# A new written order for a one-core transformer block: loads of x and Wk first, turns of Wq later, five reciprocals on ScalarE

## The chip, the core and the metric

The kernel runs on one core of a Trainium2 chip. A core has five engines that each work through their own list of instructions and meet only at semaphores: TensorE (PE in the profile; its weight loads are PEld), VectorE (DVE), ScalarE (ACT), GpSimd (POOL) and SyncE (SP), which here issues most of the DMAs. An engine's DMA issues are marked with a q (SPq, ACTq). SBUF is the on-chip memory, PSUM the eight banks into which TensorE writes. The metric is the time of one execution in microseconds (us).

## The reference

One block of a transformer over 2048 tokens of width 640. The first half is linear attention with a feature map, the second a gated MLP; both have a layer norm ahead and a residual behind.

```python
x = A_x
h = x + _A_ref(_layernorm(x), A_wqkv, A_w_phi, A_wo)
h2 = h + _B_ref(_layernorm(h), B_w_gate, B_w_up, B_w_down)

# _A_ref, 32 heads of width 20
pq = einsum("bhsd,hdf->bhsf", q, w_phi);  pk = einsum("bhsd,hdf->bhsf", k, w_phi)
phi_q = concat([softmax(pq), softmax(-pq)]);  phi_k = concat([softmax(pk), softmax(-pk)])
kv = einsum("bhsf,bhsd->bhfd", phi_k, v);  z = einsum("bhsf->bhf", phi_k)
o = einsum("bhqf,bhfd->bhqd", phi_q, kv) / (einsum("bhqf,bhf->bhq", phi_q, z)[..., None] + 1e-6)
return o.transpose(0, 2, 1, 3).reshape(B, S, D) @ wo

# _B_ref, F = 1536
return ((x @ w_gate) * (x @ w_up)) @ w_down
```

## The kernel before

The tokens are 16 tiles of 128. Every operation has a name, a letter or two and the tile's number, and the text uses these names:

- Loads: x0, x1, x3 (one tile each), x4, x6 and so on (two tiles); wk0 to wk4, wv0 to wv4 (rows of Wk and Wv, 160 KB each), w5 (the feature matrix w_phi, in 40-byte rows), wo0 and wo2 (Wo), wg and wu (rows of the MLP's gate and up weights, 384 KB each), wd0 to wd3 (quarters of the down weights, 480 KB each). All at line 282.
- Turns, which are DMAs that transpose: wqt0 to wqt4 turn Wq out of DRAM (line 306), xt turns a normalized tile of x (465), qT the features of Q (569), oT an attention output (606), hT a normalized tile of h (640). A turn's target has the layout that TensorE needs; what waits for it is the matmul that reads it. Only SP issues turns.
- The start: WT0 to WT4 turn the rows of Wk on TensorE (386, with copies WTe at 248), xt0 and xt1 turn the first two tiles of x there (456, copies xte). Ph0 to Ph2 on POOL spread w_phi to a block form Phi (374). F1_0 to F1_4 fold Phi into Wk on TensorE (405; copies Fe1 at 248), F0_0 to F0_4 do the same for Wq, once the five turns of Wq have landed. A fold of Wk needs its row's turn and all of Phi; a fold of Wq needs all five turns.
- The first half: K, V and Q are the projections (476; of tiles 0 and 1 in five parts, one for each row of the weight, as K1_0), with exponentials Kx (488) and Qx (545, 547), sums Ks (492) and Qs (550), Ln and Exp for the softmax on ACT (495, 497, 553, 560) and products Kn (512) and Qn (564) on POOL. KV is the sum over tokens (520). After the last KV, N multiplies the turned Q features with it (582); then dd (596) makes the denominator, rd (599) its reciprocal, o (602) divides, oT turns, and O multiplies with Wo (612). h (618) adds the residual, hc (626 or 627) centres it, hT turns it.
- The second half: tokens in five blocks of 256, 512, 512, 512 and 256 columns. U{block}_{tile of F}_{gate or up} are the matmuls (655), g (660) copies the gate, u (663) multiplies, D (674) is the down matmul, y (686) adds the residual, w (688) stores. L1n (437) and L2v (633) are small steps of the two layer norms.

What sets the order is a list written out by hand, or rather by a search: `PLAN` gives each operation a number on the scale of us, optionally another engine, and the PSUM banks or buffer slots that it takes. Each engine runs its operations in the order of these numbers, and waits on semaphores for what an operation reads and for the last users of the slot that it takes. A number is an order, not a time: nothing in the kernel reads a clock.

```python
k, a, o.slots = PLAN.get(name, (key, 0, ()))
...
for o in sorted(G.ops, key=lambda o: (o.key, o.i)):
    order[o.eng].append(o)
```

Two PSUM banks hold a projection, an N or an O. A matmul group that takes banks waits until the engine that reads them for the group before is done: exponentials for K and Q, o for N, h for O.

Of the kernel before, what the change touches and what calls it, by code (L numbers as in the profile page):

```python
# [54 lines left out]
WTe1:6.125:1 L1s3:6.193 xt0:6.33::0 wqt0:6.41 WT2:6.609::2 ekz:6.705 L1e1:6.71 xte0:6.808 xn1:6.98::1 WT3:7.046::3 F1_1:7.325::4 WTe2:7.391 L1a3:7.51 WTe3:7.619
WT0:7.646::6 wv0:7.72:1 L1l3:7.976 WT4:8.096::7 WTe0:8.123:1 wv1:8.2 L1e3:8.303 F1_2:8.375::0 Fe1_1:8.396 WTe4:8.573:1 L1n3:8.582 wv2:8.68:1 F1_0:8.694::2
Fe1_2:8.981 xt1:9.013::6 wv4:9.16:1 Fe1_0:9.211:1 F1_3:9.292::4 xn3:9.721::2 xte1:9.795 F1_4:9.863::0 K0_0:10.182::2 L1s5:10.251 xt3:10.359 Fe1_3:10.379
K0_1:10.453 K1_0:10.724::6 Fe1_4:10.963:1 K1_1:10.995 L1s4:11.038 K1_2:11.266 K0_2:11.537 x2:11.547:1 x10:11.669 K0_3:11.808 L1a5:11.825 L1a4:11.948 L1s7:12.057
# [4 lines left out]
L1e6:19.159 Kx3_0:19.252::2 L1s11:19.392 L1n6:19.439 rqz:19.663 V5:19.67::0 Kn0:19.7 Kx3_1:19.836 wqt4:20.023 L1a11:20.302 xn6:20.411::2 Kx5_0:20.42::3
L1s8:20.941 Kx5_1:21.004 V4:21.026::2 xt6:21.333 Kr1:21.588 L1s10:21.728 Ke1:21.879 Sz:22.013 Ve5:22.025::3 L1n7:22.192 K2:22.382::6 Kn1:22.416 L1a10:22.638
x14:22.643 xn7:22.747::0 L1l10:22.871 Ve4:23.053::4 L1a8:23.277 xt7:23.385 L1a9:23.386 Ks3:23.495::2 F0_0:23.738::4 Kx2_0:23.938::4 F0_4:24.057::0 V2:24.376::2
Kx2_1:24.522 x12:24.695 L1e10:25.106 wd0:25.175 Fe0_0:25.199 Ks2:25.258::3 V6:25.732::6 L1l8:25.783 L1e8:26.109 Ve2:26.202::5 L1n9:26.389 L1n8:26.613
L1n11:26.651:1 Kr2:26.786 L1s15:26.826 mk0:26.837 mk1:27.001 Ke2:27.077 K4:27.088::4 Fe0_4:27.223 mk2:27.346 Ve6:27.613:1:6 Kn2:27.616 xn8:27.807:1:1
xn9:28.344::3 KV0:28.444::2,3 Kr3:28.622 F0_2:28.777::0 xn11:28.874::2 Kx4_0:28.975::0 xt9:28.982 KV1:29.096 Ks5:29.404::0 K7:29.429::6 Kx4_1:29.559
L1n10:29.929 Ke3:30.143 Fe0_2:30.289 xt8:30.292 Kn3:30.477 KV2:30.785 Ks4:30.797::1 Kr5:30.916 Kx7_0:31.062::1 F0_3:31.118::4 V7:31.437::0 wu1:31.602
Kx7_1:31.646 wg0:32.082 L1s12:32.19 Kr4:32.309 wu0:32.562 Ke4:32.6 Fe0_3:32.746 K6:32.793::6 Kn4:32.934 xt11:33.042 L1a12:33.1 Ks7:33.209::3 Ve7:33.33::7  # L70
# [4 lines left out]
KV5:41.933 K11:42.266::0 Qx0_1:42.328 Qr1:42.938::0 L1e12:43.084 Ke9:43.177 L1n12:43.322:1 Kr8:43.323 L1n13:43.364 Qx5_0:43.469::2 Qb1:43.588 xn12:43.606::3
Q3:43.622::4 L1n14:43.787 Kn9:44.011 Qx5_1:44.079 L1n15:44.136:1 xn15:44.42::1 Kx11_0:44.689::3 Qs0:44.95 KV6:44.989 xt15:45.058 Kx11_1:45.273 Q9:45.322::6
Ke8:45.857 Qe1:46.003 Qx3_0:46.122::3 Qn1:46.324 wg2:46.368 Ks11:46.385::2 KV7:46.689 Qx3_1:46.732 wo0:46.848 K10:47.022::0 Qx9_0:47.342::4 Kn8:47.589
xn13:47.778::2 Qx9_1:47.952 Qs5:48.308 V8:48.378::4 xt13:48.416 Kr11:48.562 Qr0:48.708::1 Kx10_0:48.854::4 Ke11:49.438 Kx10_1:49.584 wg3:49.726 K15:49.734::6
# [8 lines left out]
Kn14:69.394 qT2:69.464::5 KV11:69.761 Qx10_0:69.959::2 V15:70.094::0 Qx10_1:70.569 wd1:70.954 Qs10:71.364 KV12:71.45 Ve15:71.65::6 Qb4:71.707 KV13:71.783
KV14:72.116 Qe4:72.234 Qr13:72.353::3 KV15:72.449 Qn4:72.541 Q6:72.782::6 KVe1:72.98 KVe0:73.23 Qb13:73.806 N0:74.149::4 Qx6_0:74.347::4 N2:74.482::0
qT4:74.673::1 dd0:74.68::0 Q7:74.815::2 rd0:74.895 Qx6_1:74.957 dd2:75.185::1 o0:75.309::0 rd2:76.064 oT0:76.177::0 N1:76.182::6 Qx7_0:76.38::3 o2:76.478::1
Q11:76.515::4 Qr10:76.99::0 Qe13:77.136 dd1:77.233::0 Qx7_1:77.255 Qn13:77.443 rd1:77.448 oT2:77.487::1 o1:77.862::2 Q8:77.882::0 Qx11_0:78.08::5 Qs7:78.617  # L90
Qx11_1:78.69 Qb10:78.708 oT1:78.797::2 N3:79.249::2 Qx8_0:79.494::0 N9:79.582::6 O0:79.915::4 Qe10:80.104 qT13:80.107::5 dd9:80.113::0 Qx8_1:80.223 rd9:80.328
dd3:80.618::1 rd3:80.833 Qr7:80.833::1 o9:81.123::0 Qb7:81.177 O2:81.273::0 Qe7:81.452 Qn7:81.759 o3:81.878::1 oT9:81.991::3 N5:82.631::6 h2:82.83 Q14:82.964::2
qT7:83.301::0 h0:83.65 L2q2:83.775 O1:84.331::0 Qs6:84.47 hc0:84.615::1 oT3:84.791::0 Qx14_0:85.333::1 O9:85.689::4 dd5:85.905::0 Qx14_1:85.943 h1:86.011
hT0:86.101 Qr6:86.553::2 rd5:86.831 Qb6:86.897 Q12:87.047::2 Qe6:87.172 h9:87.246 hc1:87.291::2 Qn6:87.479 o5:88.066::2 hT1:88.147 N4:88.414::0 Qx12_0:88.612::3
# [821 lines left out]
```

## Time and profile before

| | us |
|---|---|
| median of 3 runs | 273.67 (273.38 to 274.04) |
| the profiled execution | 272.24 |
| span of its trace | 270.5 |
| TensorE busy | 264.9 |
| DVE busy | 161.3 |
| ACT busy | 123.8 |
| POOL busy | 71.1 |
| granted TensorE clock | 1.00 |

The span runs from the first to the last instruction in the trace, and times within a trace count from its start. In a timeline a row is start, length, engine, line, operation, target from sources, shape and count; rows of one kind are merged, and a bracket tells for how long the engine was idle before and what ended that. Matmuls overlap, so their lengths add up to more than the time they take, and the distance of two starts is the better measure. In the chain of work that ended last a row is start, length and what the time went to; a DMA's row there runs from its issue to its landing. In rows of DMA issues the last two numbers are the size and the median time from issue to landing. In rows by windows the columns are the window, its length, busy time of PE, PEld, DVE, ACT and POOL with the count of instructions, the granted clock, the DMA engines' share and GB/s. In rows by groups they are the count, then busy us and mean ns of one, then idle time before.

### The profile page before, as it was taken

What the parts mean: (1) busy time and instruction counts of PE and PEld (TensorE: products, weight loads), DVE (VectorE), ACT (ScalarE), POOL (GpSimd) and SP (SyncE); (2) the same over time, 40 slices, a digit from 0 to 9 for tenths busy, and PEclk for the clock granted to TensorE, in tenths of its full rate; (3) what the DMA queues carried; (4) which work ended last, traced back from release to release, by engine and by line L of the source; (5) the groups of instructions that cost most, each with busy time, mean ns of one, the idle gap of its engine ahead of it and who ended that gap; (6) DMA issues with size and microseconds to landing.
All of it is one profiled execution on the core that took longest, in us unless ns stands there. A gap on an engine that the chain in (4) does not pass through costs nothing.

```text
span 270.5 us, 5202 instructions
## 1 busy us (share of the span) xinstructions
PE 264.9 (98%) x2105; PEld 177.9 (66%) x2105; DVE 161.3 (60%) x299; ACT 123.8 (46%) x307; POOL 71.1 (26%) x87
## 2 busy tenths in 40 slices
PE   7899999999999999999999999999999999999996
PEld 4677777777777788567456577766445467544775
DVE  4998999997789799786653434321324322333424
ACT  3799989988766564417406512440120400032000
POOL 4217889999832422330001000000000000000000
PEclk9999999999999999999999999999999999999999
DMA  6998791999979989586253205001300000200003
GB/s 169 326 200 156 178 231 54 172 263 263 199 172 156 137 163 183 104 139 118 52 121 68 55 0 76 23 4 48 73 0 15 0 0 27 73 1 0 27 0 109
DMA packets 67944, 28.09 MB, mean 104 GB/s; under 512 B 59088, under 2 KB 66640, under 8 KB 67920
## 3 DMA queue, kind: packets, MB, share of 16 engines
q1 hardware_dynamic: 66544, 26.12, 47.0%
q10 hardware_dynamic: 1376, 1.64, 2.0%
q8 instruction: 16, 0.26, 0.4%
q14 instruction: 8, 0.07, 0.1%
HBM read 11.00 MB, written 2.62 MB: 50 GB/s over the span
## 4 chain that ended last, share of the span: by engine, by line
PE 94%; DMA 2%; SPq 1%; ACT 1%; issue 0%; DVE 0%; DVEq 0%
PE ps L655 38%; PE ps L476 24%; PE ps L674 19%; PE ps L612 8%; PE ps L520 2%; PE ps L582 2%; DMA ev<-in_A_wqkv_dram 2%; PE ps L405 1%; DMA xnT<-xn 1%; PE ps L386 1%; SPq L306 0%; ACT ph L545 0%; SPq L282 0%; DVE Wp L686 0%; PE ps L456 0%
## 5 line engine op out<-in xcount | busy, mean ns | idle before, releaser
L655 PE MATMUL ps<-xnT,Wgu 128*128 128x512 bf16 (+1 forms) x600 | 108.1, 336 | 0.4 <-DMA xnT<-xn 0.4
L655 PEld LDWEIGHTS ps<-xnT,Wgu 128*128 128x128 bf16 x600 | 58.0, 98 | 43.8 <-issue 0.6
L660 ACT ACTIVATE gt<-ps 128x512 bf16<-128x512 f32 (+1 forms) x60 | 29.4, 509 | 103.1 <-PE ps L655 81.9
L476 PE MATMUL ps<-Wp,xnT 128*128 128x320 bf16 (+1 forms) x480 | 68.4, 299 | 0.0
L663 DVE TENSOR_TENSOR ev<-ps,gt 128x512 bf16<-128x512 f32 (+1 forms) x60 | 33.6, 578 | 55.3 <-PE ps L655 37.0
L476 PEld LDWEIGHTS ps<-Wp,xnT 128*128 128x128 bf16 x480 | 45.7, 97 | 17.3
L674 PE MATMUL ps<-Wd,ev 128*128 128x320 bf16 (+2 forms) x396 | 53.7, 295 | 0.0
L674 PEld LDWEIGHTS ps<-Wd,ev 128*128 128x128 bf16 x396 | 38.2, 98 | 15.0 <-DVE ev L663 0.2
L512 POOL TENSOR_TENSOR ek<-ek,SR 128x1280 bf16<-128x1280 bf16 x16 | 37.6, 2356 | 1.3 <-ACT SR L497 1.1
L686 DVE SCALAR_TENSOR_TENSOR Wp<-ps,rs,x_all 128x640 bf16<-128x640 f32 (+3 forms) x18 | 14.5, 808 | 30.3 <-PE ps L674 29.9
L550 DVE TENSOR_REDUCE S<-ph 128x66 f32<-128x1320 bf16 x16 | 24.2, 1520 | 2.4 <-ACT ph L547 2.3
L492 DVE TENSOR_REDUCE SR<-ek 128x64 f32<-128x1280 bf16 x16 | 23.4, 1467 | 1.0 <-ACT ek L488 0.9
L612 PE MATMUL ps<-Wo,Wp 128*128 128x320 bf16 x160 | 23.9, 299 | 0.0
L545 ACT ACTIVATE ph<-ps 128x600 bf16<-128x600 f32 x32 | 21.3, 689 | 5.3 <-PE ps L476 4.3
L564 POOL TENSOR_TENSOR ph<-ph,RQ 128x660 bf16<-128x660 bf16 x16 | 20.8, 1305 | 9.4 <-ACT RQ L560 9.4
L488 ACT ACTIVATE ek<-ps 128x640 bf16<-128x640 f32 x32 | 21.3, 717 | 0.8 <-PE ps L476 0.7
L612 PEld LDWEIGHTS ps<-Wo,Wp 128*128 128x128 bf16 x160 | 15.4, 98 | 6.7 <-issue 0.3
L618 DVE SCALAR_TENSOR_TENSOR x_all<-ps,x_all 128x640 bf16<-128x640 f32 x16 | 13.1, 822 | 7.5 <-PE ps L612 7.4
L629 ACT ACTIVATE ek<-x_all,mv 128x640 bf16<-128x640 bf16 x16 | 13.1, 820 | 3.5 <-DVE x_all L618 3.5
L602 DVE TENSOR_TENSOR o<-ps,sm 128x660 bf16<-128x660 f32 x16 | 13.3, 838 | 0.4
L248 ACT ACTIVATE ev<-ps 128x640 bf16<-128x640 f32 x13 | 9.2, 713 | 1.5 <-PE ps L476 1.4
L557 POOL TENSOR_TENSOR RQ<-RQ 128x32 f32<-128x32 f32 x14 | 3.3, 239 | 24.5 <-ACT RQ L553 24.4
(66 smaller groups left out, 164.0 us busy)
## 6 DMA issues: line engine op xcount, KB each, us to landing
out_dram<-Wp SPq DMA_DIRECT2D x15, 160.0 KB, 1.8
x_all<-in_A_x_dram SPq DMA_DIRECT2D x6, 320.0 KB, 4.5
...
Wp<-in_A_wqkv_dram SPq DMA_DIRECT2D x5, 160.0 KB, 4.1
ev<-in_A_wqkv_dram SPq DMA_DIRECT2D x4, 160.0 KB, 4.0
x_all<-in_A_x_dram ACTq DMA_DIRECT2D x3, 160.0 KB, 3.4
```

Of the source, the lines that this page charges most:

```text
L476: ins = e.matmul(pb(b, hb)[:, 0:n1 - n0], lhsT=T["xnT"][:, NC - 1 - c, P * t:P * (t + 1)], rhs=T["Wp"][:, POS[kind], c, n0:n1], start=(c = ...
L488: G.op("act", "%sx%d_%d" % (nm, t, s), lambda e, s=s, b=b, ek=ek: e.activation(out=T["ek"][:, ek.slots[0], 0:2 * D].rearrange("p (b h s f) ...
L492: G.op("dve", "%ss%d" % (nm, t), lambda e, ek=ek, sr=sr: e.tensor_reduce(out=T["SR"][:, sr.slots[0], 0, :], in_=T["ek"][:, ek.slots[0], 0: ...
L512: G.op("pool", "Kn%d" % t, lambda e, eng, ek=ek, sr=sr: e.tensor_tensor(out=T["ek"][:, ek.slots[0], 0:2 * D].rearrange("p (h f) -> p h f", ...
L545: e.activation(out=v[:, 0:10].rearrange("p (b g) j f -> p b g j f", b=2), in_=pp(b, 0, 300).rearrange("p b (g j f) -> p b g j f", j=3, f=D ...
L550: G.op("dve", "Qs%d" % t, lambda e, t=t, ph=ph: e.tensor_reduce(out=T["S"][:, t, 0:66].rearrange("p (g k) -> p g k", k=6), in_=pv(ph).rear ...
L564: return e.tensor_tensor(out=v, in0=v, in1=T["RQ"][:, rq.slots[0], 1, 0:33].rearrange("p (g j) -> p g j", j=3).unsqueeze(3).to_broadcast([ ...
L612: ins = e.matmul(pb(b, hb)[:, 0:320], lhsT=T["oT"][:, oT.slots[0], c, :], rhs=T["Wo"][:, c, 320 * hb:320 * (hb + 1)], start=(c == 0), stop ...
L655: ins = e.matmul(pb(b)[:, 0:n], lhsT=T["Wgu"][:, gu, c, P * ft:P * (ft + 1)], rhs=T["xnT"][:, NC - 1 - c, o0:o0 + n], start=(c == 0), stop ...
L660: G.op("act", "g%d_%d" % (bi, ft), lambda e, pg=pg, gt=gt, n=n: e.activation(out=T["gt"][:, gt.slots[0], 0:n], in_=pb(pg)[:, 0:n], func=AF ...
L663: o_ = G.op("dve", "u%d_%d" % (bi, ft), lambda e, pu=pu, gt=gt, hh=hh, ft=ft, n=n: e.tensor_tensor(out=T["hh"][:, hh.slots[0], ft, 0:n], i ...
L674: ins = e.matmul(pb(b, hb)[:, 0:w], lhsT=T["hh"][:, hh.slots[0], ft, P * tt:P * (tt + 1)], rhs=T["Wd"][:, ft, c0 + w * hb:c0 + w * (hb + 1 ...
```

## The change

The whole list `PLAN` is replaced, so that nearly every engine has another order; the matmuls, their shapes and their number stay. What the text speaks of:

- SP's first issues were wqt2, w5, x3, wk2, wk3, wk0, wk4, wv3, x4, x6, wqt0, wv0, wv1, wv2, wv4, xt3; they are x3, wk0, x1, wk1, w5, wk3, wk4, wk2, wv2, x4, wv0, x2, wv1, x6, x10, wv3, xt3, wv4, wqt2, wqt0. ACT issued x0, x1, wk1 and later x2, wo2 and wd2; it issues x0 and later wd0. The turns of Wq were at 0.8, 6.4, 12.6, 17.3 and 20.0 on the list's scale; they are at 10.3, 11.6, 16.8, 19.4 and 20.7.
- TensorE had WT1, xt0, WT2, WT3, F1_1, WT0, WT4, F1_2, F1_0, xt1, F1_3, F1_4, K0_0. It has WT0, WT1, WT3, xt0, WT2, WT4, F1_1, xt1, F1_0, F1_2, F1_4, F1_3, K1_0. The five copies Fe1 were four on ACT and one on DVE and are all on ACT; xte0 and xte1 go from ACT to DVE.
- On POOL an L1n stands between Ph0 and Ph1; several memsets go from the start to after 15.
- Wd's loads were at 25, 71, 97 and 133 and are at 32 (wd3), 58 (wd0, on ACT), 59 (wd2) and 71. xt8 stands right behind wo0 and wd3.
- Where the first half ends, TensorE had N0, N2, Q7, N1, Q11, Q8, N3, N9, O0, O2; it has N0, N2, Q7, N9, N1, Q11, N3, Q8, O0, Q14, O2. SP had hT2, qT14, oT10, hT4, hT5 ahead of block 1's first U; it has hT2, hT5, qT14, hT4, oT10.
- The reciprocal of the denominator goes from DVE to ACT for tiles 2, 5, 6, 14 and 15, as Ln and Exp of minus that. The 33rd column of the result, which is padding, is set to zero once by POOL.

```diff
+RACT = (2, 5, 6, 14, 15)
...
-gl0:0.78 wqt2:0.78 x0:0.78:1 va1:0.846 zero:0.91 warm0:1.127 x1:1.26:1 warm1:1.345 warm2:1.564 eps:1.676 id0:1.706 wk1:1.74:1 warm3:1.782 id1:1.944 warm4:2.001
-w5:2.09:1 gla:2.188 warm5:2.219 phz:2.398 warm6:2.437 x3:2.57:1 warm7:2.656 warm8:2.874::0 wk2:3.05:1 warm9:3.093 glb:3.115 warm10:3.311 warm11:3.529 wk3:3.53
...
+x3:0.78:1
...
+wk0:1.26:1
...
+w5:2.7:1
...
+F1_1:8.754::6
...
+wqt2:10.25
...
+wd3:32.33
...
+xt8:32.81
...
+hT5:99.514
...
+    init["sm"] = [G.op("pool", "smz", lambda e: e.memset(T["sm"][:, :, 1, H:H + 1], 0.0), 0.1, LP, [], [], -60.2)]
...
-        G.op("dve", "rd%d" % t, lambda e, sm=sm: e.reciprocal(out=T["sm"][:, sm.slots[0], 1, 0:33], in_=T["sm"][:, sm.slots[0], 0, 0:33]),
-             0.30, LD, [sm], [sm], kk)
+        if t in RACT:
+            G.op("act", "rl%d" % t, lambda e, sm=sm: e.activation(
+                out=T["sm"][:, sm.slots[0], 0, 0:H], in_=T["sm"][:, sm.slots[0], 0, 0:H], func=AF.Ln), 0.24, LA, [sm], [sm], kk)
+            G.op("act", "rd%d" % t, lambda e, sm=sm: e.activation(
+                out=T["sm"][:, sm.slots[0], 1, 0:H], in_=T["sm"][:, sm.slots[0], 0, 0:H], func=AF.Exp, scale=-1.0), 0.21, LA,
+                [sm], [sm], kk)
+        else:
+            G.op("dve", "rd%d" % t, lambda e, sm=sm: e.reciprocal(
+                out=T["sm"][:, sm.slots[0], 1, 0:33], in_=T["sm"][:, sm.slots[0], 0, 0:33]), 0.30, LD, [sm], [sm], kk)
```

More of the change, by code (lines that the diff above doesn't have):

```diff
@@ L55 @@
[L55 to L58, printed above, removed]
@@ L63 @@
[L63 to L66, printed above, removed]
@@ L67 @@
[L67 to L70, printed above, removed]
@@ L75 @@
[L75 to L78, printed above, removed]
@@ L87 @@
[L87 to L94, printed above, removed]
@@ new lines @@
+warm0:1.127
+warm1:1.345
+warm2:1.564
+warm3:1.782
+warm4:2.001
+warm5:2.219
+warm6:2.437
+warm7:2.656
+id0:0.78
+id1:1.018
+warm8:2.874::0
+warm9:3.093
+x3:0.78:1
+L1s3:3.725
+x0:0.78:1
+L1s0:4.512
+warm10:3.311
+warm11:3.529
+L1a3:5.299
+warm12:3.748
+warm13:3.966
+warm14:4.185
+warm15:4.403
+wk0:1.26:1
+WT0:4.846::1
+warm16:5.404
+warm17:5.622
+warm18:5.82
+gl0:1.262
+x1:1.74
+wk1:2.22
+WT1:6.096::2
+w5:2.7:1
+L1a0:5.422
+WTe0:5.602
+eps:1.329
+gla:1.425
+glb:1.728
+L1l0:6.187
+L1s1:5.531
+L1l3:6.369
@@ new lines @@
+L1a1:6.441
+ekz:1.938
+Ph0:6.225
+warm19:6.375
+warm20:6.484
+warm21:6.593
+L1e0:6.551
+xn0:6.789::0
+L1e3:6.695
+L1n3:6.975
+xn3:7.319::1
+WTe1:6.788:1
+L1l1:7.373
+L1e1:7.699
+xn1:7.937::2
+wk3:3.18
+WT3:7.146::0
+wk4:3.66:1
+xt0:7.456::3
+Ph1:7.199
+wk2:4.14:1
+WT2:8.196::4
+xte0:8.467:1
+WTe3:7.792:1
+WT4:8.475::5
+WTe2:8.673
+Ph2:7.591
+F1_1:8.754::6
+Fe1_1:9.271
+WTe4:8.952:1
+xt1:9.073::1
+xte1:9.55:1
+wv2:4.62:1
+x4:5.1
+L1s5:9.959
+F1_0:9.352::2
+F1_2:9.671::4
+Fe1_0:9.869:1
+Fe1_2:10.453:1
@@ new lines @@
+F1_4:10.032::6
+wv0:5.58:1
+F1_3:10.351::0
+Fe1_3:11.037
+L1s4:10.745
+Fe1_4:11.621:1
+L1a5:11.533
+L1a4:11.655
+K1_0:10.67::2
+K1_1:10.941
+K0_0:11.214::4
+x2:6.06
+L1s2:11.764
+wv1:6.54
+x6:7.02
+L1l4:12.205
+x10:7.5
+K0_1:11.485
+K0_2:11.756
+L1e4:12.531
+L1n5:12.769:1
+xn5:13.053::3
+K1_2:12.027
+K1_3:12.298
+wv3:7.98
+K1_4:12.569
+Kx1_0:13.039::0
+Kx1_1:13.623
+L1n4:12.811
+xn4:13.583::0
+xt3:8.46
+wv4:9.77:1
+L1a2:14.113
+L1l2:14.346
+L1e2:14.672
+L1n2:14.952
+wqt2:10.25
+K0_3:12.84
+K0_4:13.111
@@ new lines @@
+L1s6:14.222
+Ks1:15.009::0
+V1_0:13.382::0
+Kx0_0:14.765::1
+Kx0_1:15.349
+xn2:15.933:1:2
+wqt0:11.56
+va1:15.176
+xt5:13.691
+L1a6:16.402
+V0_0:13.653::6
+L1s7:16.511
+L1a7:17.421
+V0_1:13.924
+V0_2:14.195
+V1_1:14.466
+V1_2:14.737
+mk0:16.006
+mk1:16.17
+mk2:16.515
+L1s11:17.53
+K3:15.008::2
+Kx3_0:16.748::2
+Kx3_1:17.332
+V1_3:16.364
+phz:16.785
+xt4:15.001
+V1_4:16.635
+x8:16.311
+L1s10:18.317
+L1l6:17.916
+L1e6:18.242
+L1n6:18.522
+xn6:19.104::1
+wqt3:16.791
+V0_3:16.906
+V0_4:17.177
+L1a10:19.634
@@ new lines @@
+L1n7:18.746
+Kr1:18.335
+Ke1:18.626
+L1a11:19.743
+Kn1:18.97
+xt2:18.101
+Ks3:19.852::1
+V3:17.448::4
+Ve3:19.004::0
+L1l10:19.976
+L1e10:20.302
+Ve0:20.395::1
+L1n11:21.245:1
+L1n10:21.283
+wqt4:19.411
+Ve1:20.979::2
+K5:18.804::2
+Kx5_0:21.563::3
+Kx5_1:22.147
+V5:20.16::4
+wqt1:20.721
+xt6:22.031
+V4:21.516::6
+Ks0:21.42::2
+xn7:22.813::3
+xt7:23.451
+Ve4:23.072::3
+Kr0:23.656
+Ke0:23.947
+x12:24.761
+Ve5:24.093::4
+Kn0:24.281
+K2:22.872::0
+Kx2_0:24.677::4
+Kx2_1:25.261
+V2:24.228::2
+F0_4:25.584::6
@@ new lines @@
+Fe0_4:26.101
+Ve2:26.685::5
+F0_0:25.903::4
+V6:26.222::0
+xn11:23.343::0
+KV0:27.578::6,7
+L1s8:23.873
+wu0:25.241
+L1s9:24.66
+L1a9:25.57
+x14:25.721
+L1a8:25.679
+xn10:27.269:1:2
+L1l8:28.084
+Kr3:28.266
+Ks2:25.997::3
+Kr2:28.412
+Ke2:28.703
+L1e8:28.849
+L1n8:29.129
+xt10:28.222
+Ve6:27.778:1:6
+K4:27.911::2
+Fe0_0:28.942
+Kx4_0:29.526::1
+Kx4_1:30.11
+KV1:29.267
+L1n9:29.353
+Ks5:28.509::0
+xn9:29.902::1
+Sz:29.577
+xt9:30.54
+F0_2:29.6::0
+Fe0_2:30.694
+Ke3:31.278
+xn8:30.432::3
+K7:29.919::4
@@ new lines @@
+Kx7_0:31.475::0
+L1s13:30.962
+Kr5:32.059
+Kx7_1:32.205
+rqz:29.756
+wo0:31.85
+V7:31.275::2
+Ks4:31.749::2
+Ve7:32.831::7
+Ke5:33.415
+Kn2:29.793
+KV2:32.631
+F0_3:32.964::0
+L1s12:33.142
+Kr4:33.561
+Ke4:33.852
+Kn3:32.106
+Fe0_3:33.998
+K6:33.283::4
+Kx6_0:34.839::4
+Kx6_1:35.423
+F0_1:34.639::2
+wd3:32.33
+Fe0_1:36.007
+L1s15:33.929
+Ks7:34.716::3
+Kr7:36.591
+Ke7:36.882
+KV3:34.958
+Ks6:36.159::1
+K9:35.291::0
+L1a15:37.552
+Kx9_0:37.028::2
+Kx9_1:37.612
+Q1_0:36.647::4
+Q1_1:36.919
+Q1_2:37.191
@@ new lines @@
+Qx2_0:54.834::5
+Qx2_1:55.444
+Qs9:54.605
+qT5:54.824::1
+K13:54.636::4
+Kx13_0:56.192::1
+Kx13_1:56.776
+xt14:56.314
+Kr15:57.36
+Ke15:57.651
+Qs2:56.239
+Qr2:57.797::0
+Qb2:58.099:1
+Qn3:58.332
+KV9:55.992
+Kn15:59.597
+Qr9:57.943::1
+V10:56.325::0
+qT0:57.624::2
+wd0:58.089:1
+V11:57.681::2
+Ve10:58.569::5
+Ks13:59.599::0
+Ve11:59.237::0
+wd2:59.114
+K12:59.037::4
+Kx12_0:60.593::2
+Kx12_1:61.177
+KV10:60.393
+KV11:60.726
+Kr13:61.761
+Ke13:62.052
+Q4:61.059::0
+Qx4_0:62.624::0
+Qx4_1:63.234
@@ new lines @@
+KV13:72.273
+qT9:66.034::4
+Qs4:70.159
+Qr4:71.712::2
+Qs13:71.594
+Qb4:72.182
+Ve15:72.14::7
+KV14:72.606
+wg1:67.524
+KV15:72.939
+KVe0:73.47
+KVe1:74.059
+Qe4:72.724
+Qn4:73.031
+qT2:69.939::5
+Q6:73.272::4
+Qx6_0:74.837::3
+N0:74.639::2
+dd0:75.17::0
+Qx6_1:75.447
+rd0:75.385
+N2:74.972::0
+dd2:75.675::1
+Q7:75.305::6
+N9:76.672::4
+wd1:71.429
+o0:75.799::0
+qT4:75.163::2
+rl2:76.057
+rd2:76.367
+o2:76.672::1
+N1:77.005::2
+dd9:77.427::0
+dd1:77.536::2
+rd1:77.751
+oT0:76.667::0
+o1:78.165::2
@@ new lines @@
+Qr13:76.527::3
+Qb13:76.871
+Qe13:77.146
+Qn13:77.453
+Q11:77.569::0
+oT2:77.977::1
+N3:79.062::2
+Qx7_0:77.265::4
+Qx7_1:77.875
+Qx11_0:79.134::5
+qT13:79.287::5
+rd9:78.92
+Qx11_1:79.744
+Qs7:79.21
+Qr7:80.763::1
+oT1:80.777::2
+Qr10:80.909::0
+o9:80.793::0
+oT9:82.087::3
+Qb7:81.107
+Qs6:81.548
+Qe7:81.382
+Qn7:81.689
+Q8:79.395::6
+Qx8_0:81.501::0
+Qx8_1:82.111
+Qr6:83.101::2
+Qb6:83.445
+Qe6:83.72
+qT7:83.397::4
+O0:80.799::0
+dd3:82.983::0
+rd3:83.198
+o3:83.612::1
+Q14:82.157::4
+oT3:84.887::0
@@ new lines @@
+Qx15_1:98.049
+hT2:97.819
+Qs15:98.844
+u0_1:100.278
+u0_2:100.609
+hc5:98.659::1
+hT5:99.514
+U0_4_0:98.504::0
+L2v1:97.626
+g0_4:100.73::3
+qT14:100.825::1
+N10:99.05::4
+O4:99.383::2
+h4:100.941
+hc4:101.885:1:2
+U0_3_0:100.742::7
+g0_3:101.486::1
+hT4:102.459
+L2r1:102.338
+dd10:102.407::2
+U0_3_1:101.287::6
+U0_4_1:101.834::1
+u0_3:102.513
+u0_4:102.844
+rd10:103.175
+o10:103.59::2
+oT10:104.457::0
+Qr15:101.76::1
+Qb15:102.103
+U0_5_0:102.379::0
+Qe15:102.379
+Qn15:102.686
+qT15:105.767::2
@@ L143 @@
+w15_2:267.08
+smz:29.758
 """.split():
```

686 lines of the change are left out of this document (620 added, 66 removed).

## The prediction

> **What bounds the kernel now.** I read the page's shares and its chain first, then the chain, engine order and DMA landings of the first 12 us, and last the timeline of TensorE, looking for places where its starts lie further apart than the same work elsewhere.
>
> ```profile
> PE 264.9 (98%) x2105; PEld 177.9 (66%) x2105; DVE 161.3 (60%) x299; ACT 123.8 (46%) x307; POOL 71.1 (26%) x87
> PE 94%; DMA 2%; SPq 1%; ACT 1%; issue 0%; DVE 0%; DVEq 0%
> 11.18 11.03 PE L476 MATMUL ps<-Wp,xnT 128*128 128x320 bf16 x80
> ```
>
> TensorE is the bound, and the matmuls are the same before and after. Only three things can move: when the first projection starts (11.18 us), lost time between there and the last matmul, and the tail, whose order (D10, then the three cut pieces of D15, then the stores) stays. The chain of the start:
>
> ```profile
> 0.80 1.26 SPq L306
> 2.12 0.57 SPq L282
> 2.75 0.50 SPq L282
> 3.29 4.06 DMA ev<-in_A_wqkv_dram
> 8.37 0.48 PE ps L405 x6
> ```
>
> A turned Wq row (L306) is issued first on SP, though Wq is not folded until after 24 us; then Phi's w5, x3, and wk2, whose landing at 7.35 us releases TensorE. The first fold of Wk (L405) starts at 8.37 and the first projection 2.81 us later. So the start is bound by SP's order and by landings.
>
> **Part 1: the start.**
>
> ```profile
> 3.29 1.94 SPq L282 DMA_DIRECT2D ev<-in_A_wqkv_dram  x4
> ev<-in_A_wqkv_dram SPq DMA_DIRECT2D x4, 160.0 KB, 4.0
> ev<-in_A_wqkv_dram ACTq DMA_DIRECT2D x1, 160.0 KB, 3.5
> w<-in_A_w_phi_dram SPq DMA_DIRECT2D x1, 25.0 KB, 4.4
> 6.55 1.68 POOL L374 TENSOR_TENSOR Phi<-w,GL 128x160 bf16<-128x160 bf16 x3 [2.65 <-DMA w<-in_A_w_phi_dram]
> 9.12 0.26 POOL L437 TENSOR_SCALAR nb<-mv,rs 128x1 f32<-128x1 f32 x1 [0.65 <-ACT rs L433]
> 9.25 0.96 PE L405 MATMUL ps<-Phi,scratch 128*128 128x140 bf16 x12
> 10.25 0.70 ACT L248 ACTIVATE Wp<-ps 128x640 bf16<-128x640 f32 x1 [0.65 <-PE ps L405]
> 11.43 1.31 ACT L248 ACTIVATE Wp<-ps 128x640 bf16<-128x640 f32 x2
> 6.00:8.00 2.00, 1.05 (x13) 0.73 (x14) 1.44 (x4) 1.69 (x5) 1.45 (x3) 1.00 0.99 333
> 30.29 0.34 PE ps L520 x11
> 30.63 1.36 PE ps L476 x10
> 24.92 0.64 PE ps L405 x12
> 106.98 2.66 DMA xnT<-xn
> ```
>
> The new SP order is x3, wk0, x1, wk1, w5, wk3, wk4, wk2; x0 stays on ACT's queue. Four plain loads take 1.94 us to issue, 0.48 each. The last Wk row is eighth: issue at 0.80 + 7 x 0.48 = 4.2, landing 3.5 to 4.0 later, at 7.7 to 8.2. Before, wk4 was issued at 3.29 + 3 x 0.48 = 4.7 and landed at 8.7. Wk gains 0.5 to 1.0 us.
>
> But Phi is moved the other way. w5 is now fifth, issued at 0.80 + 4 x 0.48 = 2.7 instead of 2.12. With its own 4.4 it lands at 7.1, with the faster loads' 3.5 at 6.2. Behind it stand L374's 1.68 us on POOL, now with one L437 of 0.26 between its first and second part, and the 0.14 from the old Phi end (6.55 + 1.68 = 8.23) to 8.37: first fold at 6.2 + 2.1 = 8.3 up to 7.1 + 2.1 = 9.2. That L437 waits for tile 3's normalization, whose load is now first on SP.
>
> All five turns of Wk and xt0 now stand ahead of the first fold, so what follows it is shorter. Old F1_0 started half way through the pair at 9.25, at 9.72, its copy ran from 10.25 to 10.95, and the projection started at 11.18: 1.46 us. In the new order F1_0 comes after F1_1 and xt1 (0.32 + 0.28), so the projection starts 2.06 us after the first fold: 10.4 to 11.2. All five copies of folded Wk now stand on ACT, 0.61 apart (1.31 for two, less 0.70). The last is done 0.53 + 4 x 0.61 + 0.70 = 3.7 us after the first fold starts; the piece that needs it is the eighth, at 2.06 + 7 x 0.27 = 3.95. That is covered by 0.2, and each tenth that ACT slips beyond it shows on TensorE. I take first fold 8.7, projection 10.75: **minus 0.4 us**, bounds 0 and minus 0.8. The middle, since w5 no longer stands behind a turn but behind five loads. The turns of Wq go to 10 to 21 on the order's scale. The last is issued with 4.9 us of projections (three and a half of 1.36) ahead of the Wq fold; an undisturbed turn lands in 2.7 (the row at 106.98), so I cost it at nothing; each us over 4.9 would be TensorE's.
>
> The Trainium skill's page "DMA: Bandwidth & Descriptors" (Issuing engines are not separate DMA queues) says that loads from either queue run interleaved on the same 16 DMA engines, so x1 and wk1 lose only an issue slot by leaving ACT. The rows above give ACT's load 0.5 us less to land; by the rule that is its earlier place, and the bytes ahead decide. This trace does not separate the two; by the rule the sum is that of the rival on bytes below.
>
> **Part 2: lost time on TensorE after the start.**
>
> ```profile
> 80.47 0.84 PE L582 MATMUL ps<-KVm,scratch 128*128 128x63 bf16 x22
> 81.15 3.05 PE L612 MATMUL ps<-Wo,Wp 128*128 128x320 bf16 x20
> 85.74 2.88 PE L612 MATMUL ps<-Wo,Wp 128*128 128x320 bf16 x20
> 89.83 0.93 PE L582 MATMUL ps<-KVm,scratch 128*128 128x63 bf16 x22
> 90.79 1.53 PE L612 MATMUL ps<-Wo,Wp 128*128 128x320 bf16 x10
> 107.01 0.71 PE L655 MATMUL ps<-xnT,Wgu 128*128 128x256 bf16 x5
> 107.56 0.50 PE L582 MATMUL ps<-KVm,scratch 128*128 128x63 bf16 x11
> 108.79 0.71 PE L655 MATMUL ps<-xnT,Wgu 128*128 128x256 bf16 x5
> 109.89 2.43 PE L655 MATMUL ps<-xnT,Wgu 128*128 128x512 bf16 x13 [0.39 <-DMA xnT<-xn]
> ```
>
> Equal work compared: the pair O0, O2 takes 3.05 where O1, O9 take 2.88, 0.17 lost. From the start of the pair of N at 80.47 the next group starts 0.68 later, from 89.83 it starts 0.96 later: 0.28 lost, to the late turns qT7 and oT3. Five 256-wide U matmuls are 0.55 (107.01 to 107.56), so U1 could start at 109.34 and started at 109.89: 0.55 lost to hT5, issued last, at 106.98. Together 1.0 us.
>
> In the new order hT5 stands ahead of qT14, hT4 and oT10 on SP, and the Wd load that ACT issued amid those turns (wd2) stands some 40 us earlier. O2 has O0 and Q14 (2.72 us) behind Q8 in place of N3, N9 and O0 (2.04). O3 and N7 get 0.8 us more from their turn's issue. All of the 1.0 should go.
>
> What is late next: N0, N2, Q7, N9, N1, Q11 is the new order, and Q11 takes the PSUM banks that N2's division frees.
>
> ```profile
> 75.34 0.84 PE L582 MATMUL ps<-KVm,scratch 128*128 128x63 bf16 x22
> 75.88 0.19 DVE L596 SCALAR_TENSOR_TENSOR sm<-S,ps 128x33 f32<-128x33 f32 x1 [0.79 <-PE ps L582]
> 77.26 0.36 DVE L599 RECIPROCAL sm<-sm 128x33 f32<-128x33 f32 x1
> 77.65 0.84 DVE L602 TENSOR_TENSOR o<-ps,sm 128x660 bf16<-128x660 f32 x1
> 79.03 0.84 DVE L602 TENSOR_TENSOR o<-ps,sm 128x660 bf16<-128x660 f32 x1
> L495 ACT ACTIVATE SR<-SR 128x64 f32<-128x64 f32 x16 | 4.3, 272 | 0.6 <-DVE SR L492 0.6
> ```
>
> N0 starts at 75.34 and o2 ends at 78.49, 3.15 us later; the new order has 0.34 + 0.34 + 1.36 + 0.34 + 0.34 = 2.72 of TensorE there. Q11 waits some 0.4. N1's division comes 1.5 us after (79.87 less 78.49, and one more L596), Q11 covers 1.36: N3 waits 0.14, and O0 behind Q11's exponentials 0.1. New waits: 0.6, bounds 0.2 and 1.0. So part 2 is **minus 0.4**, bounds 0 and minus 0.8.
>
> **Part 3: five reciprocals to ScalarE.** For tiles 2, 5, 6, 14, 15 a DVE reciprocal of 0.36 becomes an Ln and an Exp on ACT, about 0.27 each by L495 (64 wide; these are 32). DVE loses 5 x 0.36 = 1.8 us of work and ACT gains 2.7, both under TensorE. For tile 2 the pair is queued behind Q6's two exponentials, and o2 is then free about when rd2 let it go before, so I cost it at nothing; without cover it is 0.2 per tile on the way to that tile's turn, 1.0 at most.
>
> **Sum.** 272.24 us is the profiled execution (span 270.5), 1.43 under the runs' median of 273.67. Minus 0.4 minus 0.4 gives 271.4 for a profile and **272.8** on the median. A change of 0.2% (0.55 us) is about what can be told from none.
>
> **Rivals.**
>
> *Phi holds the start.* w5 at 4.4 or more puts the projection at 11.2 and only part 2 counts: 273.2. For it: w5 is 0.6 us later on SP. Against: no turn ahead of it. 0.17.
>
> *The bank waits take all of part 2*, or turns stay late: 273.3. Against: the slack shown above. 0.10.
>
> *Bytes alone set the landings.* x0 and x3 land together at 0.8 + 3.5 = 4.3; wk0, x1 and wk1 follow 0.49 apart (164 kB at the 333 GB/s of the window from 6 to 8 us), w5 at 5.9. Fold 8.0, projection 10.1 (minus 1.1), and the bank waits at their 0.2 make part 2 minus 0.8: 271.8. Against: w5 took 4.4 here, and the Phi chain may not be the only one. 0.12.
>
> *Slower: a turn of x behind moved loads.* wd3 and wd2 (480 KB each) go from past 98 us into 32 to 60, and xt8 is issued right behind wo0 and wd3.
>
> ```profile
> DMA to landing us min/median/max: 2.6/3.9/6.0
> ```
>
> Between its place and K8 stand two KV products, two Wq folds, K6, K9 and eight fifths of a Q pair: 0.68 + 0.64 + 2.72 + 2.18 = 6.2 us, where the old order had 8.4. The nine x turns from 24 to 58 landed in at most 6.0. Beyond 6.2 each us is TensorE's; the change ends slower by 0.55 when it lands in 7.6 or later, 274.3. 0.09.
>
> *Slower: the clock.*
>
> ```profile
> 7.40 0.89 PE L386 MATMUL ps<-ident,ev 128*128 128x128 bf16 x10 [0.56 <-DMA ev<-in_A_wqkv_dram]
> 1.12 1.89 PE L361 MATMUL ps<-ev 128*128 128x256 bf16 x8 [1.12 <-DVE ev L359]
> ```
>
> The first 256-wide matmuls were 0.21 apart (1.89 less 0.42, over 7) against 0.11 for U: half speed. If the waits for six landings in turn brought that back for as long again, 3 us of projections would cost 1.5 more: 274.3. With TensorE busy 1.05 of the 2 us from 6 on and idle up to 0.56 at a time the full pace held, and the new order has more of it there. 0.04. "TensorE: Matmul & The Clock Gate" (Part 1) in the Trainium skill puts the fall at an idle window of about 3.4 us; by that rule it will not happen.
>
> **How the numbers follow.** The forecast has 0.48, its own range 272.2 to 273.3. Faster by over 0.2% is it and the bytes: 0.60. Within 0.2%: Phi and the banks, 0.27. Slower: 0.13. The range 271.9 to 274.0 leaves out the slower cases' far part and the end of the bytes.
>
> **What would show it.** First L405 near 8.7, first L476 near 10.75; no idle TensorE before the first 512-wide U; a gap of 0.4 before the Q group behind N1; DVE's L599 eleven times; the same tail. A first L476 past 11.2, or K8 waiting for an x turn, proves me wrong.

## The result, and the profile after

| | before | changed |
|---|---|---|
| median, us | 273.19 (272.01 to 274.32, 20 executions) | 272.30 (271.65 to 273.18, 20 executions) |
| the profiled execution, us | 272.24 | 272.45 |
| span of its trace, us | 270.5 | 270.7 |

The changed kernel takes 0.9966 of the time before, with a 95% interval of 0.9952 to 0.9979: 0.9 us less. The two profiled executions do not show it: that of before lies 0.95 under its median, that of the changed kernel 0.15 above its own. A difference of two single traces is therefore not the effect of this change, and part of the study goes to what a second and third trace of the same kernel show.

The shares on the page of the changed kernel, to hold against the prediction's first fence:

```profile
PE 265.8 (98%) x2105; PEld 178.7 (66%) x2105; DVE 158.6 (59%) x291; ACT 126.8 (47%) x320; POOL 71.3 (26%) x88
PE 87%; DMA 5%; DVE 4%; ACT 2%; SPq 1%; issue 1%; DVEq 0%; ACTq 0%
```

TensorE's work is the same, DVE lost 2.7 us of work and ACT gained 3.0. On the chain of the end, DMA went from 2% to 5%. Its DMA pieces, with what follows each, in the order of time (start, length, what it went to):

```profile
4.20 4.03 DMA ev<-in_A_wqkv_dram
...
8.27 0.47 PE ps L1328 x5
...
22.68 4.05 DMA xnT<-xn
...
26.77 1.53 PE ps L1418 x10
...
87.01 4.41 DMA Wp<-o
91.47 1.53 PE ps L1561 x10
```

The first is wk2, the second the turned row of x tile 6, the third the turned row oT3. The timeline of TensorE at the start of the changed kernel, from 22 to 30 us, and where the first half ends; start, length and idle time as in the earlier fences:

```profile
8.27 0.73 PE L1328 MATMUL ps<-ident,ev 128*128 128x128 bf16 x10 [0.54 <-DMA ev<-in_A_wqkv_dram]
8.84 0.48 PE L1347 MATMUL ps<-Phi,scratch 128*128 128x140 bf16 x6
9.16 0.44 PE L1398 MATMUL ps<-ident,xn 128*128 128x128 bf16 x5
9.44 1.49 PE L1347 MATMUL ps<-Phi,scratch 128*128 128x140 bf16 x24
10.77 2.48 PE L1418 MATMUL ps<-Wp,xnT 128*128 128x320 bf16 x17
...
25.73 0.80 PE L1347 MATMUL ps<-Phi,scratch 128*128 128x140 bf16 x12
26.77 1.53 PE L1418 MATMUL ps<-Wp,xnT 128*128 128x320 bf16 x10 [0.25 <-DMA xnT<-xn]
...
76.06 1.53 PE L1418 MATMUL ps<-Wp,xnT 128*128 128x300 bf16 x10
77.42 0.84 PE L1524 MATMUL ps<-KVm,scratch 128*128 128x63 bf16 x22
78.37 1.54 PE L1418 MATMUL ps<-Wp,xnT 128*128 128x300 bf16 x10
79.84 0.51 PE L1524 MATMUL ps<-KVm,scratch 128*128 128x63 bf16 x11
80.19 1.53 PE L1418 MATMUL ps<-Wp,xnT 128*128 128x300 bf16 x10
...
90.07 0.50 PE L1524 MATMUL ps<-KVm,scratch 128*128 128x63 bf16 x11
90.88 0.51 PE L1524 MATMUL ps<-KVm,scratch 128*128 128x63 bf16 x11 [0.32 <-DMA scratch<-ph]
91.47 1.53 PE L1561 MATMUL ps<-Wo,Wp 128*128 128x320 bf16 x10
92.83 1.53 PE L1418 MATMUL ps<-Wp,xnT 128*128 128x300 bf16 x10
...
106.94 3.54 PE L1604 MATMUL ps<-xnT,Wgu 128*128 128x256 bf16 x25
```

What is lost is read from distances of starts, as in the prediction; it is worked out from unrounded starts, so that the rounded rows give up to 0.01 more or less. The two Wq folds (twelve L1347) take 0.64 and the projection behind them starts 1.04 after them: 0.41 lost, to tile 6. A Q group takes 1.36; from 76.06 it is 1.36 to the next, and the pair of N there takes 0.68 but 0.95 pass until Q11: 0.26 lost; from 78.37 to N3 1.47 pass, 0.11 lost. One N takes 0.34; 0.81 pass at 90.07 and 0.59 at 90.88: 0.47 lost to qT7 and 0.25 to oT3. In the stretch from 106.94, which holds block 1's first 512-wide U, 0.13 is lost. The sum is 1.6 us, where the prediction counted 1.0 in the kernel before and forecast 0.6 here.

### The profile page after: what moved, and what is told of

The parts are those of the page before. It is cut to its first block, busy times and chain, and to the rows that moved or that the text cites. A ratio compares the mean times of both kernels' runs of the same rounds, so it can differ in the third digit from the quotient of the medians.

```text
span 270.7 us, 5200 instructions
## 1 busy us (share of the span) xinstructions
PE 265.8 (98%) x2105; PEld 178.7 (66%) x2105; DVE 158.6 (59%) x291; ACT 126.8 (47%) x320; POOL 71.3 (26%) x88
## 4 chain that ended last, share of the span: by engine, by line
PE 87%; DMA 5%; DVE 4%; ACT 2%; SPq 1%; issue 1%; DVEq 0%; ACTq 0%
PE ps L1604 38%; PE ps L1623 19%; PE ps L1418 18%; PE ps L1561 8%; PE ps L1462 2%; DMA Wp<-o 2%; DMA xnT<-xn 1%; DMA ev<-in_A_wqkv_dram 1%; PE ps L1524 1%; SPq L1223 1%; ACT Wp L1189 1%; DVE SR L1434 1%; DVE xn L1389 1%; DVE st L1365 1%; DVE st L1364 1%
## 5 line engine op out<-in xcount | busy, mean ns | idle before, releaser
L1582 POOL TENSOR_SCALAR ln<-mv 128x1 f32<-128x1 f32 x9 | 1.7, 191 | 91.0 <-ACT ek L1578 90.6
```

## The experiments

Each experiment changes numbers of `PLAN`, but for one that changes `RACT`. Ratios are to the kernel before.

### Wq's turn first again

```diff
 the changed kernel
-wqt2:10.25
+wqt2:0.775
```

> The changed kernel with one thing undone: the first turn of Wq (wqt2) stands again ahead of all loads on SP. Everything that SP issues up to 10.5 us comes 1.26 us later, wk2 lands at 9.5 instead of 8.2 and the first projection starts at 12.0 instead of 10.8. My theory (the start reaches the end): 1.2 us slower than the changed kernel, ratio to before about 1.001. Rival 1 (a later wait for xt6, whose turn comes off a full SP queue, absorbs the start; it was 0.4 us in the changed kernel's trace): 0.8 us slower, ratio 0.9995, and the wait ahead of V6 is gone. Rival 2 (the start is worth nothing): ratio stays 0.9966.

Measured 274.25 us (12 executions, 273.01 to 275.26), ratio 1.0023 (0.9996 to 1.005). The chain of this run:

```profile
0.80 1.25 SPq L1247
...
5.66 3.87 DMA ev<-in_A_wqkv_dram
...
9.57 0.47 PE ps L1328 x5
```

One turn ahead of the loads costs an issue of 1.25 and moves wk2's landing from 8.23 to 9.53; the first projection starts at 12.07 in place of 10.77. With that one number the changed kernel loses all it had gained: 1.95 us on the median for 1.3 us of start. In the changed order the late turn of Wq is necessary. The profiled execution is the shortest of its twelve, so that no trace shows where the 0.65 us beyond the start went.

### Only Wq's turn late

```diff
 the kernel before
-wqt2:0.78
+wqt2:10.2
```

> The kernel before with one thing done: wqt2 moved from the front of SP's queue to behind the loads of Wv. Loads behind it come 1.26 us earlier, w5 lands near 5.2, the first projection starts near 10.1. My theory: 1.0 us faster than before, ratio 0.996, as much as the whole change. Rival 1 (absorbed by the wait for a turn of x up to V6, which comes off SP one at a time): ratio 0.999 to 1.000 with V6 still at 26.7. Rival 2 (the gain of the change is in the later turns alone): ratio 1.000.

Measured 273.37 us, ratio 1.0004 (0.9978 to 1.003). The first projection started at 10.50, 0.68 earlier than in the first trace of before, and nothing of it reached the end: the first 512-wide U started later than before, at about 110.39 instead of 109.89. Its rows on TensorE, the first weight load of the U group, then SP's turns ahead of it:

```profile
108.22 0.71 PE L655 MATMUL ps<-xnT,Wgu 128*128 128x256 bf16 x5
110.61 1.57 PE L655 MATMUL ps<-xnT,Wgu 128*128 128x512 bf16 x9 [1.68 <-DVE ev L663]
```

```profile
110.36 0.56 PEld L655 LDWEIGHTS ps<-xnT,Wgu 128*128 128x128 bf16 x4 [1.72 <-issue]
```

```profile
101.00 3.44 SPq L569 DMA_TRANSPOSE scratch<-ph  x1
...
105.81 2.92 SPq L640 DMA_TRANSPOSE xnT<-xn  x2
```

The distance of the two rows is 2.39 where five 256-wide matmuls take 0.55, which reads as 1.84 lost. But this trace lacks 14 of the 2105 matmul records, and the group's first is one of them: two weight loads stand ahead of the row at 110.61, which is therefore the second matmul, and 512-wide matmuls are 0.22 apart. So the group started at about 110.39 and lost 1.62. (The traces of three other runs, those of the sections above and below this one, lack 15 each; a gap of 0.22 there is a missing record and not a wait.) The row names DVE's L663, the last thing to end before, but by the kernel's order this U group waits for hT5 and for a PSUM bank that an earlier L663 had freed at 108.5. hT5 is the second of the L640 pair and landed at 110.15; it stands behind qT14, whose issue alone took 3.44 us here and 2.35 in the first trace of before. ACT issues wd2's 480 KB just ahead of that, at 98.3.

### wd1 earlier, and the reciprocals back on DVE

```diff
 the changed kernel
-wd1:71.429
+wd1:41.0
 the changed kernel, another run
-RACT = (2, 5, 6, 14, 15)
+RACT = ()
```

> The changed kernel with one load moved: wd1 (480 KB) goes from 71 to 41 on the list's scale, away from the turn qT4, whose issue took 2.4 us behind it. My theory (that load holds up SP, and every turn up to O3 is issued 1 us late): qT4's issue takes 1.5, oT0 is issued 1 us earlier, the waits of N7 and O3 (0.7 us together) fall to 0.2 or less: 0.5 to 0.7 us faster than the changed kernel, ratio 0.9945. Rival (qT7 and oT3 land late, 5.4 and 4.4 us after their issue, because of the turns beside them): waits and ratio as in the changed kernel, 0.9966.

Measured 272.53 us, ratio 0.9971 (0.9949 to 0.9992). N7's wait is gone, that at O3 stayed at 0.26, and the median did not improve. In this execution wk2 landed at 8.64 and the start was 11.18, later than in the unedited kernel's trace, though nothing ahead of it was edited.

> The changed kernel with the five reciprocals back on DVE, the rest of the order kept. My theory (both engines lie under TensorE there): within 0.2 us of the changed kernel, ratio 0.996 to 0.9975. Rival (DVE is the narrow one around the first N, 1.8 us of work goes back to it): 0.4 to 1.0 us slower, ratio 0.998 to 1.000, with longer waits of Q11, N3 and O3.

Measured 272.45 us, ratio 0.9978 (0.9954 to 1.0001). Q11's wait grew from 0.26 to 0.48, and its row in the list of waits then names the division:

```profile
PE ps L1418 <- DVE o L1551: 0.3, 1, 0.3
```

The changed kernel's interval (0.9952 to 0.9979) lies almost whole within this one, so five reciprocals on ScalarE are worth nothing that these runs can tell; the 0.2 at Q11 is what the trace has for them. This execution had no wait at V6 and none at N7, though wd1 and the turns of Wq stand where the changed kernel has them: these two waits, too, come and go.

### Only wd2 early, and both edits together

```diff
 the kernel before
-wd2:97.429:1
+wd2:41.0
 and in the second run also
-wqt2:0.78
+wqt2:10.2
```

> The kernel before, with one edit: the load of wd2 (ACT's queue, planned at 97.4) is issued from SP at about 41 us, with the other weights, as the changed kernel does in spirit. Theory (the load stretches the turns that feed block 1's first U, and this wait is longer in most executions than the 0.55 us of the profiled one; the run with Wq late had 1.84 there): the start stays at 11.2, the first 512-wide U waits less than 0.2, ratio 0.996 to 0.998. Rival (the gain comes from the start alone): ratio 0.999 to 1.001. Rival (the wait goes but the next turn behind it on SP, for oT14 or hc4, is late instead): a wait of 0.4 or more at a later U or N, ratio 0.999 to 1.001.

Measured 272.75 us, ratio 0.9972 (0.995 to 0.9995): this one edit gives about 0.7 of the 0.9 us, with an interval of 0.1 to 1.4. The first 512-wide U started at 109.59 and lost 0.07. qT14's issue still took 2.40, but oT10's behind it 1.28 in place of 1.83, and hT5 landed at 109.35.

> The kernel before, with two edits and nothing else: Wq's last-third turn late (planned at 10.2) and wd2 loaded at about 41 us. Theory (start and wd2 are in series: the start's gain is lost at the first 512-wide U as long as wd2 is loaded amid its turns): first projection at 10.5, no wait over 0.2 at that U, ratio 0.992 to 0.995, so faster than the changed kernel. Rival (SP's turns in the middle of the kernel are the limit whatever the load does, so an earlier start is lost there): first projection at 10.5, but waits of 0.5 or more for qT, oT or hT turns between 75 and 115 us, ratio 0.996 to 0.998, that is what moving wd2 alone gives. Rival (Wq's late turns cost something in the first 30 us): a wait at V6 or F0 of 0.4 or more.

Measured 272.47 us, ratio 0.9968 (0.9946 to 0.999). The two edits together are not faster than wd2's alone by anything that the intervals can tell; the expected 0.992 to 0.995 is a miss, and the ratio is that of the first rival, though no single wait reached the 0.5 that it asked for. The trace says why it tells little of the start. Its chain:

```profile
1.88 4.81 DMA ev<-in_A_wqkv_dram
...
6.73 0.47 PE ps L386 x5
```

wk1, from ACT's queue, took 4.81 to land, and the first projection started at 11.04, not at the 10.5 of the run with Wq's turn alone. And the first 512-wide U lost 0.34 again: with hT5 landing at 109.33, SP's turns take back what TensorE had gained before them.

### The changed kernel with wd2 back

```diff
 the changed kernel
-wd2:59.114
+wd2:97.429:1
```

> The changed kernel with wd2's load put back to ACT's queue at 97.4, all else as in the changed kernel. Theory (the load amid the turns takes the start's gain): a wait of 0.5 to 1.5 at the first 512-wide U or at the O and N just before it, ratio 0.999 to 1.002. Rival (the changed order of the heads leaves enough slack there, so the load's place is not what counts): no such wait, ratio 0.996 to 0.997 as the changed kernel itself.

Measured 272.49 us, ratio 0.9969 (0.9947 to 0.9991), and no wait at the first 512-wide U. The theory that wd2's place carries the gain falls for the changed order. There hT5 is issued ahead of qT14, hT4 and oT10; in this trace it landed at 107.46, and hT4, now the last turn of that U, at 110.14, 0.54 ahead of the U's start at 110.68. By this reading the two parts are alternatives, and each takes the last turn out of the load's way; the order of hT5 alone was not tried in the kernel before.

The profiled execution was the longest of its twelve, 273.92 us, and shows another loss. Its chain from 8 us:

```profile
8.58 7.89 DMA xnT<-xn
...
16.52 1.53 PE ps L1418 x10
```

The turn of x tile 3 landed 7.89 us after its issue, against 5.48 in the first trace of the changed kernel, and K3 lost 1.46.

### wd1 early, and tile 6's turn ahead of Wq's

```diff
 the changed kernel
-wd1:71.429
+wd1:41.0
-wqt1:20.721
+wqt1:22.0
-xt6:22.031
+xt6:20.8
```

> The changed kernel with two edits: wd1's load at 41 us in place of 71.4, and the turn of x tile 6 issued ahead of the turn wqt1 on SP. Theory (V6's wait of 0.41 and N7's of 0.47 are paid on the path): both under 0.1, xt6 landed at about 25.5, ratio 0.993 to 0.995. Rival (every wait that is removed shows up at the next late transfer, as O3's 0.26 stayed when wd1 alone was moved): V6 and N7 gone, but O3, Q11 or the first U take 0.5 or more, ratio 0.996 to 0.997.

Measured 273.08 us (272.22 to 275.17), ratio 0.9995 (0.997 to 1.002), slower than theory and rival expected. V6's wait went and a new one came one group earlier:

```profile
21.81 4.24 PE L1418 MATMUL ps<-Wp,xnT 128*128 128x320 bf16 x30
26.39 0.80 PE L1347 MATMUL ps<-Phi,scratch 128*128 128x140 bf16 x12 [0.35 <-issue]
```

The Wq fold now waits 0.51 for the turn wqt1, which landed at 26.30. Wq's late turns and tile 6's stand back to back on SP, and whichever comes last is late. The profiled execution was the shortest of twelve; why the others reach 275.17 no trace shows.

### Second looks at both kernels

No edit: the kernel before twice more, the changed kernel once more.

> The kernel before, unchanged, profiled once more. Theory (its median lies 0.9 us above its first profiled execution because turned rows that land with 0.2 to 0.55 us to spare in that execution land too late in others): if this execution takes over 273, waits of 0.3 or more for xt3 at V3, for xt5 at K5 or for hT5 at the first 512-wide U, over 0.8 in sum beyond the 1.0 of the first profile; if it takes under 272.5, the same waits as in the first profile. Rival (slower executions are slower everywhere, by clock or by the pitch of matmuls): no new wait, and the end later by a longer stretch after 130 us.

> The same kernel once more, as the second look: the theory expects the time above 272.2 to be found in the first 30 us (wk2, xt3, xt5) and at the first 512-wide U (hT5), the rival after 130 us.

> The changed kernel, unchanged, profiled once more. Theory: xt3 lands 1.0 or so before K3 wants it and xt5 over 1.0 before K5, so no wait there unless xt3 takes over 6.5 us; the waits at V6 (0 to 0.45), Q11 and N3 (0.37 together), N7 and O3 (0.7 together) as in the first profile, within 0.3; time 271.8 to 272.8. Rival (the changed kernel's executions differ as much as those of before): waits that come and go by over 0.5 in the first 30 us, time up to 273.5.

The second look at before took 274.05 us, the third 272.09. TensorE's timeline of the second:

```profile
10.97 5.59 PE L476 MATMUL ps<-Wp,xnT 128*128 128x320 bf16 x40
16.88 2.89 PE L476 MATMUL ps<-Wp,xnT 128*128 128x320 bf16 x20 [0.32 <-DMA xnT<-xn]
19.97 1.26 PE L476 MATMUL ps<-Wp,xnT 128*128 128x320 bf16 x8 [0.19 <-DMA xnT<-xn]
...
109.59 0.71 PE L655 MATMUL ps<-xnT,Wgu 128*128 128x256 bf16 x5
111.71 2.00 PE L655 MATMUL ps<-xnT,Wgu 128*128 128x512 bf16 x11 [1.41 <-DVE ev L663]
```

SP's turns ahead of that U, and then the L640 group of its trace, with its first and last start and the time to landing:

```profile
101.99 3.77 SPq L569 DMA_TRANSPOSE scratch<-ph  x1
105.80 1.28 SPq L606 DMA_TRANSPOSE Wp<-o  x1
107.12 2.93 SPq L640 DMA_TRANSPOSE xnT<-xn  x2
```

```profile
L640 SPq DMA_TRANSPOSE xnT<-xn x2: 1210/1244/1277, 107.1 to 108.8; - x2
DMA to landing us min/median/max: 2.6/2.7/2.7
```

V3 lost 0.48 to tile 3's turn, K5 0.35 to tile 5's, both with no loss in the first look, and U 1.57 (2.12 less 0.55): hT5 issued at 108.8 landed at 111.47. Those three are 1.85 more than in the first look, which had 0.55 at U alone, and N7 and O3 lost 0.16 more; the start was 0.21 earlier. That gives 1.8, the whole of 274.05 less 272.24. The rival, a later end without new waits, falls: clock 1.00, and the waits account for it. The third look had 0.35 at K5 and 0.91 at U, with a start of 10.56.

The second look at the changed kernel took 272.85:

```profile
10.23 4.51 PE L1418 MATMUL ps<-Wp,xnT 128*128 128x320 bf16 x32
15.88 5.33 PE L1418 MATMUL ps<-Wp,xnT 128*128 128x320 bf16 x38 [1.14 <-DMA xnT<-xn]
```

Its start was 0.54 earlier than in the first look and K3 lost 1.30, as tile 3's turn took 7.2 us. The waits at Q11, N3, N7 and O3 came out as in the first look (0.26, 0.11, 0.50, 0.26). So my theory was half right: these stay, but the early turn that I thought safe is not, and the case that it had set aside (over 6.5 us to land) came at once. The rival's waits that come and go in the first 30 us are what this trace shows.

### The load of tiles 10 and 11 behind tile 3's turn

```diff
 the changed kernel
-x10:7.5
+x10:10.3
-wd1:71.429
+wd1:41.0
```

> The changed kernel with x tile 10 loaded behind the turns of x tile 3 and of Wq's third part, and wd1 at 41 us. Theory (what is left of the spread is xt3 against K3 and wv4 against V1 in the first 17 us): xt3 lands 0.4 to 0.7 earlier, its margin at K3 1.4 or more, median 272.1 to 272.4, no execution over 273.2, ratio 0.994 to 0.997. Rival (the spread comes from later transfers, or x10 is late for its own LayerNorm): median 272.4 to 273, executions up to 273.8, a wait on ACT at x10's sum.

Measured 271.57 us (6 executions, 271.24 to 272.00), ratio 0.9933 (0.9912 to 0.9953). That is 1.9 us under the 273.45 that the kernel before took beside it, the least of all kernels here, and less than the theory expected. Of this kernel's turn of tile 3 the group row and its time to landing, and TensorE at the start:

```profile
L1407 SPq DMA_TRANSPOSE xnT<-xn x1: 1310/1310/1310, 8.1 to 8.1; - x1
DMA to landing us min/median/max: 4.9/4.9/4.9
```

```profile
10.74 10.50 PE L1418 MATMUL ps<-Wp,xnT 128*128 128x320 bf16 x76
```

The turn is issued an issue slot earlier (8.07 for 8.58) and takes 4.9 where the unedited kernel took 5.5 and 7.2. It lands 2.15 us before K3 wants it, against 1.07 in the first look at the changed kernel, and TensorE runs from the first projection to 21 us without a gap. Here, too, there was no wait at V6. The run with wd1's move alone differs from this one only in x10, and its ratio was 0.9971; the intervals just overlap, and one trace shows the landing, so that x10's part is likely and not shown. The page "DMA: Bandwidth & Descriptors" of the Trainium skill (Issuing engines are not separate DMA queues) says that all DMAs end up on the same 16 engines and interleave there. By that rule x10's 320 KB were what the turn had to share the engines with; the shorter landing in this one trace agrees.

## Why the prediction was right, and where its terms were not

It forecast 272.8 us, faster, in a range of 271.9 to 274.0; it was 272.30. Most of this 0.5 is the base: the prediction started from the 273.67 of three runs, and twenty have a median of 273.19. The change itself was forecast as minus 0.8 and measured as minus 0.9.

That came close, but not by the prediction's own terms. For a profiled execution it forecast 271.4, and the first look had 272.45: the start gave the 0.4, but the lost time behind it went from 1.0 to 1.6 us instead of to 0.6. So the agreement on the median is in good part luck.

The prediction's two kinds of term, the start and the time lost behind it, were complete, though. In each of the fourteen traces, the time of the execution, less the start of the first projection, less the time that TensorE lost behind it, comes to 260.0 to 260.1 us, whatever the order. What differs between executions and kernels is the start and the waits alone.

**The start.** Predicted first fold 8.7 and first projection 10.75; the first look had 8.84 and 10.77. The size was right. The gate was not, in that execution: Phi was said to hold the fold, but w5 landed at 6.07, Phi was done at 8.07, and what released TensorE was the landing of wk2 at 8.23, at the late end of the predicted 7.7 to 8.2. In the second look it was Phi: wk2 landed at 7.49, POOL's last part of Phi ended at 8.10, and the fold followed.

```profile
7.03 1.07 POOL L1316 TENSOR_TENSOR Phi<-w,GL 128x160 bf16<-128x160 bf16 x2
```

```profile
8.25 0.48 PE L1347 MATMUL ps<-Phi,scratch 128*128 128x140 bf16 x6
```

The run with the reciprocals on DVE has the same (wk2 at 7.94, Phi until 8.70, fold at 8.84). So the two gates lie close together and change places from one execution to the next. The rival in which Phi holds the projection back to 11.2 did not come out: where Phi was the gate, the projection started at 10.23 and 10.77. The start is not one number: 11.18, 10.97 and 10.56 in three looks at before, 10.77 and 10.23 in two at the changed kernel. The means differ by 0.4, as forecast; the second look comes close to the 10.1 of the rival on bytes.

**"An undisturbed turn lands in 2.7, so I cost it at nothing."** Wq's turns between 10 and 23 us were not undisturbed: they stand back to back on SP with those of x, landed in 3.7 to 6.0 and put tile 6's turn 0.41 late at V6 in the first look, not at all in the second. Over all traces of the changed order the term is 0 to 0.54.

**"All of the 1.0 should go."** Half right. O2's 0.17 went, and the first U's 0.55 became 0.13 and 0.15. But N7 and O3, 0.28 before, lost 0.72 and 0.76. The prediction gave them 0.8 us more from their turns' issue, which is what the numbers of `PLAN` say; in the first looks N7's place on TensorE came 5.26 us after qT7's issue before and 4.97 after, so that SP's lateness took all of it. The early wd1 left 0.06 to 0.11 of N7's loss and did not touch O3's; but two of the traces with wd1 in its old place have no wait at N7 either.

**New bank waits.** Predicted Q11 0.4, N3 0.14, O0 0.1; measured 0.26, 0.11, 0. Mechanism and place right, the size 0.3 too large.

**The reciprocals** at nothing: no run contradicts it.

**What was mis-sized is the wait at the first 512-wide U.** The prediction took its 0.55 from one execution, and that was one of the shortest. Four traces with wd2 in its old place and the old order of turns have 0.55, 0.91, 1.57 and 1.62 there. Not all of this is a loss of its own: in the third look and in the run with Wq late, TensorE came to that U some 0.5 earlier than in the first look and waited there for hT5, so that the wait took back what the start had gained. The U itself started at 109.89, 109.77, 111.71 and 110.39. The step "minus 0.4 minus 0.4 on the median" treated the 1.43 us between trace and median as a constant that both kernels share. It is not: the second look finds the difference of the kernel before in waits, over half of it at a place that the change repairs. That this under-counted gain made up for N7, O3 and V6 fits the medians, but no run shows it by itself.

How much of the 0.9 us each place gives is not settled. The three looks at before average 272.79 us and the two at the changed kernel 272.65, closer than the medians; five traces are too few for the split. Shown by medians: wd2's move alone gives the kernel before about 0.7 (0.1 to 1.4); Wq's late turn alone gives it nothing (between 0.6 faster and 0.8 slower); in the changed order wd2's place gives nothing that can be told, and the late Wq turn is worth 1.95.

**The slower rivals.** xt8 landed 4.6 us after its issue, under the 6.2 that were free; the granted clock was 1.00 in every trace.
